# Two more tiles transposed by DMA, stores held a slot longer, and the last tile finished half by half

## The chip, the cores and the metric

The kernel runs on one core of a Trainium2 chip. The metric is the device time of one execution in microseconds (us); the time before is the median of four runs. The other times are from one execution that was taken with the hardware profiler. Engines are named as in the profile: PE is TensorE (PEld its weight loads), DVE is VectorE, ACT is ScalarE, POOL is GpSimd, SP is SyncE. SP computes nothing here: it issues nearly all the DMAs, strictly in program order, and the profile shows those issues as SPq.

## The reference, cut to what matters

Inputs are q, k and v of shape (4, 8, 768, 64): batch, heads, positions, head size. Per batch and head a decayed state is carried over the positions:

```
state = gamma[None, :, None, None] * state + np.einsum('bhd,bhe->bhde', k[:, :, t], v[:, :, t])
y[:, :, t] = scale * np.einsum('bhd,bhde->bhe', q[:, :, t], state)
```

The heads are put side by side, which gives x of shape (4, 768, 512), and x goes through a block that mixes the positions and then the channels:

```
theta = x @ w_theta
zr = x * cos(theta)
zi = x * sin(theta)
y = einsum('ts,bsd->btd', w_tok_r, zr) + einsum('ts,bsd->btd', w_tok_i, zi)
u = x + y
out = u + maximum(u @ w_ch, 0)
```

The change lies in the last two lines: `u`, its product with `w_ch`, and the store of `out`.

## The kernel before, in words

**Tiles and slots.** The first half works on pairs of 128 positions: three pairs per batch, n = 0 to 11. The second half works on tiles of 128 positions: six per batch, m = 0 to 23. The two halves are interleaved by hand in one program order: after a prologue, the loop at line 592 runs slots n = 3 to 12. Slot n computes the recurrence of pair n, finishes pair n-1, and does the position mixing (`moe_M`) of the one or two tiles in `tiles_of[n]`, called `mine`. The tiles of the slot before, `done`, get their product with `w_ch` (`moe_O`) and their output (`moe_out`). From slot 7 on there are two tiles a slot: 6 and 7 in slot 7, 8 and 9 in slot 8, 10 and 11 in slot 9, and so on to 16 and 17 in slot 12. Tiles 18 to 22 follow in the loop at line 719, and tile 23 in `moe_last` (line 407).

**The way of one tile.** `moe_M` (line 327) is 12 products of 128x512 into PSUM. `moe_u` (344) adds x on DVE and leaves `u` in bf16, with five buffers. `moe_O` (365) needs `u` transposed, as its weights, and there are two ways to get that. `moe_U` (355) transposes on PE: four 128x128 products a tile against the identity, then one ACT copy from PSUM (line 361). `moe_U_dma` (350) issues one DMA transpose from SP, with four buffers `uT`. The constant `U_DMA` (line 63) says from which slot the second way is taken: in a slot n >= `U_DMA` the second tile of `done` is sent to DMA at the head of the slot (604); in a slot n with n+1 >= `U_DMA` the first tile of `mine` is sent in the middle (666); in a slot n < `U_DMA` both tiles of `done` go through PE (676). Before, `U_DMA` is 9, so tiles 6 and 7 are the last to be transposed on PE, in slot 8. `moe_O` of the tiles of `done` stands at the end of each slot (708). `moe_out` (372) takes the maximum and the sum on DVE into `ot`, which has eight buffers.

**SP's order in a slot.** Slots 8 and 9 look like this on SP: the DMA transposes of k and q of the next pair (`flip_dma`, 598 and 600); from slot 9 on the `u` of the second tile of `done`; the transpose of x of pair n-1 (`x_dma`, 638); the loads of k, q and v of pair n+3 (640, 642 and 662; pair 11, loaded in slot 8, is the last); the stores that `stores_in(n)` names (663); the `u` of the first tile of `mine` (666). Nothing overtakes on SP.

**Stores.** `stores_in` (583) gives every slot its stores. Slots 6 to 8 store nothing; slots 9, 10 and 11 store tiles 3 to 5, 6 to 8 and 9 to 11; slot 12 stores 12 and 13. With eight buffers of `ot`, the `moe_out` of tile m waits for the store of tile m-8.

**The last tile.** `moe_last` splits tile 23. The columns 0 to 383 of `u` are transposed first and columns 384 to 511 last (`flip_u`: PE, then an ACT copy, line 430). The output is made in two halves of 256 columns, e = 0 and 1, each a sum over four products (j = 0 to 3), of which j = 3 needs the last ACT copy. Before, PE runs j = 0 to 2 of both halves and then j = 3 of both (446 to 451). DVE then finishes half 0 and half 1 (454); SP issues the store of half 0 and ACT that of half 1.

Of the kernel before, what the change touches and what calls it, by code (L numbers as in the profile page):

```python
# [32 lines left out]
def kernel(  # L33
# [17 lines left out]
    nc = tc.nc  # L51
    B, H, S, D = q.shape
# [3 lines left out]
    nT = S // P  # L56
    nD = dm // P
# [2 lines left out]
    gammas = [1.0 - 2.0 ** (-5.0 - h) for h in range(H)]  # L60
    nG = nT // 2

    K_DMA, Q_DMA, X_DMA, U_DMA = 2 * nG + 1, 3 * nG - 1, 2 * nG - 1, 3 * nG

    ctx.enter_context(tc.manual_schedule())

# [89 lines left out]
    wch = const.tile([P, nD, dm], BF)  # L156
# [193 lines left out]
    def moe_U_dma(m):  # L350
        uT = work.tile([P, nD, P], BF, name="uT", bufs=4)
        nc.sync.dma_start_transpose(out=uT, in_=mo[m]["u"])
        mo[m]["uT"] = uT
# [11 lines left out]
    def moe_O(m):  # L365
        o_ps = psum.tile([P, dm], FT, name="o_ps", tag="tr", bufs=2)
        for j in range(nD):
            nc.tensor.matmul(o_ps, mo[m]["uT"][:, j, :], wch[:, j, :], start=(j == 0),  # L368
                             stop=(j == nD - 1))
        mo[m]["o"] = o_ps  # L370

    def moe_out(m):
        b, t0 = divmod(m, nT)
        ot = work.tile([P, dm], FT, name="ot", bufs=8)
        nc.vector.scalar_tensor_tensor(ot, mo[m]["o"], 0.0, mo[m]["u"], ALU.max, ALU.add)  # L375
        mo[m]["ot"] = ot

    def store(m):
        b, t0 = divmod(m, nT)
        nc.sync.dma_start(out=out[b, t0 * P:(t0 + 1) * P, :], in_=mo[m]["ot"])  # L380
# [26 lines left out]
    def moe_last(m):  # L407

        b, t0 = divmod(m, nT)
        cut = (nD - 1) * P  # L410
        cols = (slice(0, cut), slice(cut, dm))
        y_ps = [psum.tile([P, cut], FT, name="y_ps", tag="y", bufs=1),
                psum.tile([P, P], FT, name="y_ps", tag="acc", bufs=2)]
        u = work.tile([P, dm], BF, name="u", bufs=5)
        uT = work.tile([P, nD, P], BF, name="uT", bufs=4)

        def prods(e):
            for s0 in range(nT):
                for r in range(2):
                    nc.tensor.matmul(y_ps[e], wT[r][:, s0, t0 * P:(t0 + 1) * P],  # L420
                                     zs[b][:, s0, r, cols[e]],
                                     start=(s0 == 0 and r == 0),
                                     stop=(s0 == nT - 1 and r == 1))
            nc.vector.tensor_add(u[:, cols[e]], y_ps[e], xs[b][:, t0, cols[e]])

        def flip_u(lo, hi):
            u_ps = psum.tile([P, hi - lo, P], BF, name="u_ps", tag="tr", bufs=2)
            for j in range(lo, hi):
                nc.tensor.transpose(u_ps[:, j - lo, :], u[:, j * P:(j + 1) * P], ident)  # L429
            nc.scalar.copy(uT[:, lo:hi, :], u_ps)  # L430

        moe_U_dma(m - 1)
        prods(0)
        moe_O(m - 2)
        moe_out(m - 2)
        store(m - 2)
        prods(1)
        flip_u(0, nD - 1)
        moe_O(m - 1)
        moe_out(m - 1)  # L440
        store(m - 1)
        flip_u(nD - 1, nD)
        hw = dm // 2
        o_ps = [psum.tile([P, hw], FT, name="o_ps", tag="st", bufs=1),
                psum.tile([P, hw], FT, name="o_ps", tag="acc", bufs=2)]
        for js in (range(nD - 1), (nD - 1,)):
            for e in range(2):
                for j in js:
                    nc.tensor.matmul(o_ps[e], uT[:, j, :],
                                     wch[:, j, e * hw:(e + 1) * hw], start=(j == 0),  # L450
                                     stop=(j == nD - 1))
        for e in range(2):
            ot = work.tile([P, hw], FT, name="oh", bufs=2)
            nc.vector.scalar_tensor_tensor(ot, o_ps[e], 0.0, u[:, e * hw:(e + 1) * hw],
                                           ALU.max, ALU.add)
            (nc.sync, nc.scalar)[e].dma_start(
                out=out[b, t0 * P:(t0 + 1) * P, e * hw:(e + 1) * hw], in_=ot)
# [125 lines left out]
    def stores_in(n):  # L583

        if n < 2 * nG:
            return tiles_of[n - 2]
        if n < 3 * nG:
            return []
        lo = 2 * nG - 3 + 3 * (n - 3 * nG)
        return range(lo, min(lo + 3, (B - 2) * nT + 2))  # L590

    for n in range(nG, B * nG + 1):
        mine, done = tiles_of[n], tiles_of[n - 1]
# [69 lines left out]
        for t in stores_in(n):  # L663
            store(t)
# [54 lines left out]
    for m in range(last_m - nT + 1, last_m):  # L719
# [8 lines left out]
        moe_M(m, 4, nT)  # L728
        moe_u(m)
    moe_last(last_m)  # L730
# [1 line left out]
_INS = ['q', 'k', 'v', 'moe_w_theta', 'moe_w_tok_r', 'moe_w_tok_i', 'moe_w_ch']  # L732
# [26 lines left out]
```

## Time and profile before

| what | us |
|---|---|
| median of four runs | 168.44 (167.81 to 169.4) |
| the profiled execution, its own time | 168.7 |
| its span in the trace | 167.0 |
| PE busy in the span | 156.9 (94%) |
| DVE, ACT, POOL busy | 101.8, 79.1, 64.9 |
| granted PE clock over the span | 1.0 |
| slot 8, from its first product to slot 9's | 87.37 to 98.75 |
| slot 9 | 98.75 to 109.22 |

How to read it: a time in the trace is counted from the start of the span. PE products overlap in the records, so the cost of a product in a row of products is the distance between two starts, not its own duration. The chain of waits lists what the end of the program hung on, piece by piece; there the pieces don't overlap and add up. An SPq duration is the time that SP spent on issuing that one DMA; when the data has landed is a separate figure, counted from the start of the issue.

### The profile page before, as it was taken

The page shows a single profiled execution, that of the slowest core. Times are in us where ns is not written, and L with a number is a line of the kernel's source. Part 1 is how long each engine was busy: PE and PEld are TensorE (multiplying, and loading weights), DVE is VectorE, ACT ScalarE, POOL GpSimd, SP SyncE. Part 2 cuts the span into 40 slices and gives each one's busy share as a digit, 9 for nine tenths or more (in the row PEclk, how much of TensorE's full clock was granted, in tenths as well). Part 3 has the DMA queues.
Part 4 walks back from the last instruction along what each step waited for, and adds up shares of the span by engine and source line. Part 5 has one row for each costly group of instructions (what it writes and reads, how often), then busy time and mean ns, then how long its engine had stood idle before and what let it go on. Part 6 is the DMA issues. An engine that isn't in the chain of part 4 may idle for free.

```text
span 167.0 us, 4640 instructions
## 1 busy us (share of the span) xinstructions
PE 156.9 (94%) x1959; PEld 87.5 (52%) x1959; DVE 101.8 (61%) x137; ACT 79.1 (47%) x137; POOL 64.9 (39%) x82
## 2 busy tenths in 40 slices
PE   6979897899899999999999999999999999999991
PEld 2445665664566666555555554555545444444460
DVE  2358896988686599929446464584554736334442
ACT  7216568461809557587846827447083350000010
POOL 6374859787396876681632704400000000000000
PEclk9999999999999999999999999999999999999999
DMA  4999999999999999999999999968977161743343
GB/s 129 302 345 307 326 294 363 298 331 315 310 304 304 296 294 331 307 214 278 194 225 286 162 261 205 211 181 165 271 128 195 31 188 31 227 121 96 105 139 137
DMA packets 68901, 38.45 MB, mean 230 GB/s; under 512 B 26256, under 2 KB 63376, under 8 KB 68880
## 3 DMA queue, kind: packets, MB, share of 16 engines
q1 hardware_dynamic: 68736, 38.02, 88.7%
q8 instruction: 15, 0.25, 0.7%
q10 hardware_dynamic: 144, 0.13, 0.2%
q14 instruction: 6, 0.05, 0.1%
HBM read 25.69 MB, written 6.29 MB: 192 GB/s over the span
## 4 chain that ended last, share of the span: by engine, by line
PE 66%; DMA 16%; SPq 9%; DVE 4%; issue 1%; POOL 1%; ACT 1%; DVEq 0%
PE y_ps L340 31%; PE o_ps L368 12%; DMA pair<-in_k_dram 9%; PE th_ps L312 8%; DMA pair<-in_q_dram 7%; SPq L81 5%; PE yT_ps L231 3%; PE at_ps L208 2%; PE yT_ps L245 2%; PE st_ps L262 2%; SPq L95 2%; PE y_ps L420 2%; PE kq_ps L183 1%; POOL kqb L171 1%; SPq L89 1%
## 5 line engine op out<-in xcount | busy, mean ns | idle before, releaser
L340 PE MATMUL y_ps<-z,wtr 128*128 128x512 bf16 x138 | 52.4, 380 | 0.7 <-DVE z L322 0.7
L340 PE MATMUL y_ps<-z,wti 128*128 128x512 bf16 x138 | 52.3, 379 | 0.0
L347 DVE TENSOR_TENSOR u<-y_ps,x_sb 128x512 bf16<-128x512 f32 x23 | 15.8, 689 | 26.9 <-PE y_ps L340 26.7
L215 DVE TENSOR_TENSOR at<-at_ps,maskp 128x1024 bf16<-128x1024 f32 x24 | 29.3, 1221 | 4.4 <-PE at_ps L208 4.4
L175 POOL TENSOR_TENSOR kqb<-pair,qscp 128x512 bf16<-128x512 f32 x17 | 18.4, 1098 | 30.3 <-DMA pair<-in_q_dram 30.3
L175 POOL TENSOR_TENSOR kqb<-pair,vscp 128x512 bf16<-128x512 f32 x24 | 25.8, 1097 | 5.4 <-DMA pair<-in_v_dram 4.8
L285 ACT CAST xT<-yT_ps 128x512 bf16<-128x512 f32 x20 | 13.5, 737 | 30.0 <-PE yT_ps L231 30.0
L375 DVE SCALAR_TENSOR_TENSOR ot<-o_ps,u 128x512 f32<-128x512 f32 x23 | 15.9, 691 | 13.6 <-PE o_ps L368 13.4
L312 PE MATMUL th_ps<-wth,xT 128*128 128x512 bf16 x96 | 23.3, 379 | 0.1
L368 PE MATMUL o_ps<-wch,uT 128*128 128x512 bf16 x92 | 22.8, 379 | 0.3 <-DVE ot L375 0.3
L340 PEld LDWEIGHTS <-wti 128*128 128x128 bf16 x138 | 13.5, 98 | 13.8 <-issue 0.6
L276 ACT CAST stbd<-st_ps 64x256 bf16<-64x256 f32 x40 | 14.7, 367 | 12.7 <-PE st_ps L262 12.2
L340 PEld LDWEIGHTS <-wtr 128*128 128x128 bf16 x138 | 13.5, 98 | 13.7
L315 ACT ACTIVATE cs<-th_ps,halfpi 128x512 bf16<-128x512 f32 x24 | 16.5, 688 | 7.3 <-PE th_ps L312 6.8
L322 DVE TENSOR_TENSOR z<-cs,x_sb 128x1024 bf16<-128x1024 bf16 x24 | 17.7, 760 | 0.1
L316 ACT ACTIVATE cs<-th_ps,zerob 128x512 bf16<-128x512 f32 x24 | 16.5, 687 | 0.0
L312 PEld LDWEIGHTS <-xT 128*128 128x128 bf16 x96 | 9.0, 98 | 10.6 <-ACT xT L285 0.6
L368 PEld LDWEIGHTS <-uT 128*128 128x128 bf16 x92 | 8.8, 98 | 10.4 <-issue 0.4
L430 ACT COPY uT<-u_ps 128x384 bf16<-128x384 bf16 (+1 forms) x2 | 0.7, 372 | 25.5 <-PE u_ps L429 25.5
L208 PE MATMUL at_ps<-kqT 64*64 64x128 bf16 x384 | 10.6, 221 | 2.0 <-DVE at L215 1.3
L187 DVE COPY kqT<-kq_ps 128x1024 bf16<-128x1024 bf16 x14 | 9.6, 687 | 4.6 <-PE kq_ps L183 4.4
L183 PE MATMUL kq_ps<-ident,kqb 128*128 128x128 bf16 x120 | 9.5, 222 | 1.7 <-DVE wtr L400 0.6
(61 smaller groups left out, 167.1 us busy)
## 6 DMA issues: line engine op xcount, KB each, us to landing
pair<-in_k_dram SPq DMA_DIRECT2D x12, 512.0 KB, 6.6
pair<-in_q_dram SPq DMA_DIRECT2D x12, 512.0 KB, 7.5
pair<-in_v_dram SPq DMA_DIRECT2D x12, 512.0 KB, 8.3
out_dram<-ot SPq DMA_DIRECT2D x23, 256.0 KB, 2.4
wtok<-in_moe_w_tok_r_dram SPq DMA_DIRECT2D x6, 384.0 KB, 6.3
wtok<-in_moe_w_tok_i_dram SPq DMA_DIRECT2D x6, 384.0 KB, 5.6
w<-in_moe_w_theta_dram SPq DMA_DIRECT2D x1, 1024.0 KB, 8.0
w<-in_moe_w_ch_dram SPq DMA_DIRECT2D x1, 1024.0 KB, 7.6
```

The lines of the kernel that those rows point to most:

```text
L175: engines[two].tensor_mul(dst[:, two], src[:, two], _bcast_last(sc[:, 2 * g + two], D))
L208: nc.tensor.matmul(at_ps[half, par, j, :], kT[rows, two, j, half], qT[rows, :, j, half], start=(j == 0), stop=(j == NP - 1), skip_group_ch ...
L215: nc.vector.tensor_mul(at.rearrange("p a j t -> p (a j) t"), at_ps.rearrange("p a j t -> p (a j) t"), _bcast_mid(maskp[:, two].rearrange(" ...
L276: nc.scalar.copy(stbd[(c + 1) % 2][sl, :, sl], st_ps[b][sl])
L312: nc.tensor.matmul(th_ps, st[n, "xT"][:, a, j, :], wth[:, j, :], start=(j == 0), stop=(j == NP - 1))
L315: nc.scalar.activation(cs[:, 0, :], th_ps, AF.Sin, bias=halfpi, scale=1.0)
L316: nc.scalar.activation(cs[:, 1, :], th_ps, AF.Sin, bias=zerob, scale=1.0)
L322: nc.vector.tensor_mul(zs[b][:, c], st[n, "cs", a], _bcast_mid(xs[b][:, c, :], 2))
L340: nc.tensor.matmul(y_ps, wT[r][:, s0, t0 * P:(t0 + 1) * P], zs[b][:, s0, r, :], start=(s0 == 0 and r == 0), stop=(s0 == nT - 1 and r == 1))
L347: nc.vector.tensor_add(u, mo[m]["y"], xs[b][:, t0, :])
L368: nc.tensor.matmul(o_ps, mo[m]["uT"][:, j, :], wch[:, j, :], start=(j == 0), stop=(j == nD - 1))
L375: nc.vector.scalar_tensor_tensor(ot, mo[m]["o"], 0.0, mo[m]["u"], ALU.max, ALU.add)
```

## The change

Three edits. `U_DMA` becomes 8: tile 6 is sent to DMA in the middle of slot 7, tile 7 at the head of slot 8 after the transposes of k and q, and the PE transposes with their ACT copy in slot 8 go away. Slot 9 stores nothing; slots 10 and 11 store four tiles each (3 to 6 and 7 to 10) and slot 12 three (11 to 13). In `moe_last` half 0 gets its four products first and then half 1.

```diff
-    K_DMA, Q_DMA, X_DMA, U_DMA = 2 * nG + 1, 3 * nG - 1, 2 * nG - 1, 3 * nG
+    K_DMA, Q_DMA, X_DMA, U_DMA = 2 * nG + 1, 3 * nG - 1, 2 * nG - 1, 3 * nG - 1
...
-        for js in (range(nD - 1), (nD - 1,)):
-            for e in range(2):
-                for j in js:
-                    nc.tensor.matmul(o_ps[e], uT[:, j, :],
-                                     wch[:, j, e * hw:(e + 1) * hw], start=(j == 0),
-                                     stop=(j == nD - 1))
+        for e in range(2):
+            for j in range(nD):
+                nc.tensor.matmul(o_ps[e], uT[:, j, :],
+                                 wch[:, j, e * hw:(e + 1) * hw], start=(j == 0),
+                                 stop=(j == nD - 1))
...
-        if n < 3 * nG:
+        if n <= 3 * nG:
             return []
-        lo = 2 * nG - 3 + 3 * (n - 3 * nG)
-        return range(lo, min(lo + 3, (B - 2) * nT + 2))
+        lo = 2 * nG - 3 + 4 * (n - 3 * nG - 1)
+        return range(lo, min(lo + 4, (B - 2) * nT + 2))
```

SP's order around the change, before and after (the two `u` transposes that are new are marked with a star):

```
slot 7   before  k8 q8 x6 load10(k q v)            after  k8 q8 x6 load10(k q v) u6*
slot 8   before  k9 q9 x7 load11(k q v) u8         after  k9 q9 u7* x7 load11(k q v) u8
slot 9   before  k10 q10 u9 x8 out3 out4 out5 u10  after  k10 q10 u9 x8 u10
slot 10  before  k11 q11 u11 x9 out6 out7 out8 u12 after  k11 q11 u11 x9 out3 out4 out5 out6 u12
slot 11  before  u13 x10 out9 out10 out11 u14      after  u13 x10 out7 out8 out9 out10 u14
slot 12  before  u15 x11 out12 out13 u16           after  u15 x11 out11 out12 out13 u16
```

## The prediction

> **What bounds the kernel now.** I read the page's first rows and the chain of waits, then the slots one by one, then SP's own timeline. The page says who is busy:
>
> ```profile
> PE 156.9 (94%) x1959; PEld 87.5 (52%) x1959; DVE 101.8 (61%) x137; ACT 79.1 (47%) x137; POOL 64.9 (39%) x82
> ...
> PE 66%; DMA 16%; SPq 9%; DVE 4%; issue 1%; POOL 1%; ACT 1%; DVEq 0%
> ```
>
> PE is busy 94% of the span; the DMA and SPq shares of the chain lie before 45 us. From there on PE has almost no gap, so a piece taken off PE is worth its length and a wait put on PE costs its length. Busy time of PE, PEld, DVE, ACT and POOL in slots 8 to 11 (the columns after the length):
>
> ```profile
> 87.37:98.75 11.38, 11.38 (x154) 6.24 (x153) 6.25 (x9) 7.03 (x12) 4.09 (x4) 1.00 1.16 232
> 98.75:109.22 10.47, 10.47 (x125) 5.28 (x124) 6.24 (x9) 5.53 (x9) 4.05 (x4) 1.00 1.15 230
> 109.22:120.15 10.93, 10.93 (x145) 5.79 (x144) 6.25 (x9) 5.07 (x10) 0.00 (x0) 1.00 0.81 202
> ```
>
> PE fills each of them. Slot 8 has slot 10's PE work plus the PE transposes, and is 0.45 longer. The chain inside slot 8 shows the piece that goes:
>
> ```profile
> 94.15 0.45 PE u_ps L359 x8
> 94.59 2.59 PE y_ps L340 x12
> 97.18 1.73 PE o_ps L368 x8
> ```
>
> SP's timeline from the loads of pair 10 (slot 7) to the x transpose in slot 9; start, duration of the issue:
>
> ```profile
> 83.91 0.57 SPq L81 DMA_DIRECT2D pair<-in_k_dram  x1
> ...
> 87.10 3.33 SPq L195 DMA_TRANSPOSE kqT<-kqb  x1
> 90.54 2.75 SPq L195 DMA_TRANSPOSE kqT<-kqb  x1
> 93.38 1.26 SPq L290 DMA_TRANSPOSE x_sb<-xT  x1
> 94.69 0.57 SPq L81 DMA_DIRECT2D pair<-in_k_dram  x1
> ...
> 97.41 3.77 SPq L352 DMA_TRANSPOSE uT<-u  x1
> 101.29 1.52 SPq L195 DMA_TRANSPOSE kqT<-kqb  x1
> 102.92 1.25 SPq L195 DMA_TRANSPOSE kqT<-kqb  x1
> 104.26 1.24 SPq L352 DMA_TRANSPOSE uT<-u  x1
> 105.59 1.27 SPq L290 DMA_TRANSPOSE x_sb<-xT  x1
> ```
>
> One issue follows the next within 0.1 us: SP has no slack here, and a DMA put in pushes all that stands behind it. The issue at 104.26 is u9 (tile 9's u), which slot 9's second output product needs: its weight load is the fifth of these eight.
>
> ```profile
> 107.28 1.61 PEld L368 LDWEIGHTS <-uT 128*128 128x128 bf16 x8
> ```
>
> Spacing (1.61 - 0.10)/7 = 0.216, so that load begins at 107.28 + 4 x 0.216 = 108.14. u9 lands 2.5 us after its issue began (the DMA answer), at 106.76: PE arrives 1.38 later and doesn't wait.
>
> **Part 1a, off PE.** Eight transposes in slot 8: 8 x 0.056 (start to start) = 0.45, the piece above and the difference of slots 8 and 10. Taken: -0.45. The ACT copy of 1.01 us goes too, at no gain: ACT is idle 3.15 us in the next wait. Does another wait take the place? The products of tile 9 would start at 93.98 + a little instead of 94.43, and their PSUM is free when DVE has read tile 8, at 93.04 + 0.69 = 93.73; slot 10 has the same order without transposes, and no gap. So the 0.45 reaches the end of slot 8.
>
> The Trainium skill, "TensorE: Matmul & The Clock Gate", Part 4 (PE-mode transpose), gives about 275 ns for a transpose inside a kernel; eight would be 2.2 us, an estimate that would make this part -2.2. The rows decide: one lasts 219 ns but the next starts 56 ns later.
>
> **Part 1b, onto SP.** u6 goes in at about 87.1, ahead of k9 and q9; u7 behind q9; x7, load 11, u8, k10, q10 and u9 are all behind them. How far are they pushed (call it D)? Upper bound: two issues at the unhindered 1.24 plus 0.09 between issues = 2.66. Lower bound: the first transpose after a set of loads lasts 3.3 to 3.8 us whatever it is, and ends 6.5 after the first load began (83.91 to 90.43, 94.69 to 101.18). In slot 9 that one is u8, and k10 and q10 then take 1.52 and 1.25 instead of 3.33 and 2.75: from the first load to the end of q it is 9.48 with a u in between and 9.38 without. So u6 costs 0.1; if u7 were absorbed too, D = 0.1. I take the row that is the same sequence: load, u, k, q, u, x is slot 9's now, and would be slot 8's. From first load to x it took 105.59 - 94.69 = 10.90; slot 8's without the two u took 93.38 - 83.91 = 9.47. D = 1.43.
>
> The rule of the Trainium skill, "DMA: Bandwidth & Descriptors", section "Issuing engines are not separate DMA queues", says that a sequencer's time to initiate a DMA is usually small beside the DMA itself. By it D would be near 0 and the sum -0.38. The row speaks against it: 1.24 of issue in 2.5 to landing.
>
> Who waits, then? Slot 8: u7 is issued at 83.91 + 9.57 = 93.48 and lands at 95.98; its weight load comes at 96.81 + 0.86 - 0.45 = 97.22. Covered by 1.2 (by nothing at D = 2.66). u6, at 87.1 + 6.8 (u8's landing now), lands at 93.9, wanted at 96.36. k9 and q9 are wanted at 98.6 and land by about 97. Load 11: POOL's q of pair 11 now starts at 102.32, would be 1.4 later and end by 108, wanted by SP at 111. x7 and x8 are late by D for DVE's z, which slots 10 and 11 use microseconds later.
>
> Slot 9: u9 is issued at 104.26 + D and lands at 106.76 + D. A reader starts 0.11 after a landing (q of pair 10 landed at 90.64, POOL began at 90.75): 106.87 + D. PE is there at 108.14 - 0.45 = 107.69. So PE waits D - 0.82; with D = 1.43, +0.61. This is the new wait; behind it on PE is all the rest.
>
> **Part 2, stores.** Slot 9's stores leave SP between x8 and u10: 106.91 to 110.08, 3.17 us. This more than returns D, so from u10 on SP runs about 1.7 earlier than now. In slot 10 four stores instead of three (0.4 to 0.6 more) are covered by that 1.7; in slot 11 by SP's gap before u14 (stores end at 125.35, next issue 126.54); in slot 12 by that before u16 (135.55 to 137.00). New wait: ot of tile 11 needs the store of tile 3, now in slot 10, at about 115.0, plus the slowest landing of these stores, 4.3: 119.3, against DVE's 120.35. Without that cover DVE's z and mask would wait behind it, which PE doesn't need for 3 us. Part 2: 0 (0 to +0.3).
>
> **Part 3, the end.** PE, ACT and DVE in the last tile:
>
> ```profile
> 162.34 1.04 PE L449 MATMUL o_ps<-wch,uT 128*128 128x256 bf16 x8
> 162.54 0.27 ACT L430 COPY uT<-u_ps 128x128 bf16<-128x128 bf16 x1 [0.55 <-PE u_ps L429]
> 163.30 0.76 DVE L454 SCALAR_TENSOR_TENSOR oh<-o_ps,u 128x256 f32<-128x256 f32 x2
> ```
>
> Products start 0.108 apart. Now six cover the copy, which ends at 162.81, and the seventh starts at 162.99. After, three cover it: the fourth needs the copy, a hand-over (0.06) and its weight load (0.10), so 162.97; half 0 ends as now. Half 1's four follow: the last starts at 163.40 (now 163.10) and ends at 163.71. DVE begins half 1 at 163.64 now. +0.07. Bounds: -0.02 (half 0's gain) to +0.32 (three products, nothing hidden).
>
> **Sum.** -0.45 + (D - 0.82, if positive) + 0.07. At D = 1.43: +0.23. The profiled execution took 168.7 (span 167.0, 1.7 around it) and would take 168.9; the median of the runs stands 0.26 lower, at 168.44, and becomes 168.7.
>
> **Rivals.**
> A, the transposes ride free: D below 0.82, PE never waits, the sum is -0.45 + 0.07 = -0.38 and the time 168.1. For it: u8 cost SP 0.1 net in slot 9. Against it: the DMA engines are almost idle from 92.5 to 93.5 and SP still issues, so u7's 1.3 has no transfer to hide behind.
> B, slower: both pay SP's full price. D = 2.66, PE waits 1.84 for u9, sum +1.46, time 169.9. For it: SP has no gap from 77 to 107. Against it: k10 and q10 got shorter behind u8. It crosses zero at D = 1.20, and one per cent (1.68) at D = 2.88, which needs a longer issue than the unhindered ones.
> C, the end: D as forecast, but the copy's hand-over is as slow as part 3's upper bound, 0.32 instead of 0.07; the sum is +0.48 and the time 168.9. For it: three covering products are gone. Against it: ACT and DVE start 0.04 after PE's ends (162.50 to 162.54).
>
> **How the numbers follow.** Forecast (D from 0.9 to 2.0, a small new wait in slot 9; sum -0.3 to +0.8, 168.1 to 169.2): 0.52. A: 0.20. B (D above 2.0): 0.18. C: 0.07. Other: 0.03. Range: from A less 0.2 for the medians' scatter, 167.9, to B, 169.9. One per cent, 1.7 us, is about what a measurement of this kernel tells from no change. Slower by more needs D above 2.88, a part of B: 0.06. Faster by more has no case, as the whole piece is 0.45: 0.02. Within: 0.92.
>
> **What would show it.** Slot 8 about 10.93 long with no transposes in it: part 1a. x7's issue at 94.8 and load 11 at 96.1: D. A gap on PE of about 0.6 in slot 9 in the middle of the output products, ended by the uT transpose: the new wait. No such gap: A. A gap of 1.8, or one already in slot 8 before tile 7: B. u10's issue near 108.4 instead of 110.08: part 2. DVE's second half of the last tile starting 0.07 later relative to the first: part 3. I am wrong if PE waits anywhere else, for instance at slot 10's first products for k10 or q10, which land at about 107.6 against 109.1.

## The result, and the profile after

The changed kernel takes 169.38 us (median of 44 runs, 167.76 to 171.32), the kernel before 168.45 (63 runs). The ratio is 1.0032, 95% interval [1.0017, 1.0046]: 0.54 us slower, 0.29 to 0.77, counted on 168.45. That is inside the forecast's range and inside one per cent. (The ratio compares runs on the same chip and leaves disturbed runs out, so it isn't the quotient of the two medians.)

The profiled execution took 169.96, with a span of 168.2. Part of that has nothing to do with the change. Let a slot begin where the chain of waits has the four products of line 245 at its head. Slot 8 begins at 88.41, before at 87.53: 0.88 later, although the program up to that place does the same work. So I compare from the start of slot 8 on. Busy time by slot, 8 to 11; the columns are length, PE, PEld, DVE, ACT, POOL, PE clock, DMA share, GB/s:

```profile
88.41:99.34 10.93, 10.93 (x147) 5.78 (x145) 6.25 (x8) 6.12 (x11) 4.09 (x4) 1.00 1.16 205
99.34:110.53 11.19, 10.65 (x127) 5.20 (x125) 6.25 (x8) 5.53 (x9) 4.05 (x4) 1.00 1.12 226
110.53:121.46 10.93, 10.93 (x147) 5.77 (x145) 6.34 (x8) 5.08 (x10) 0.00 (x0) 1.00 0.90 204
121.46:132.39 10.93, 10.93 (x147) 5.79 (x145) 6.25 (x8) 5.07 (x10) 0.00 (x0) 1.00 0.79 151
```

With the same boundaries slots 8 to 11 were 11.38, 10.48, 10.93 and 10.93 before. Slot 8 lost 0.45 and slot 9 gained 0.71; PE, which had no gap in slot 9 before, is now idle there (10.65 busy of 11.19). Slots 10 and 11 are untouched. The chain of waits in slot 9 now leaves PE and goes over SP and a DMA:

```profile
104.89 0.05 PE st_ps L262 x3
...
105.02 0.36 ACT stbd L276
...
105.49 1.25 SPq L195
106.73 0.05 issue
106.83 2.62 DMA uT<-u
109.44 0.05 issue
109.49 1.04 PE o_ps L368 x4
```

Line 368 at 109.49 is the output product of tile 9, and the DMA ahead of it is u9. The list of waits gives the weight load's wait and the product's:

```profile
PEld L368 <- DMA uT<-u: 1.0, 1, 1.0
...
PE o_ps L368 <- DMA uT<-u: 0.5, 1, 0.5
```

The loads themselves, to be held against the row of eight at 107.28 in the prediction:

```profile
107.71 0.74 PEld L368 LDWEIGHTS <-uT 128*128 128x128 bf16 x4
109.49 0.55 PEld L368 LDWEIGHTS <-uT 128*128 128x128 bf16 x4 [1.03 <-DMA uT<-u]
```

SP's timeline of the same stretch, start and duration of each issue:

```profile
84.87 0.58 SPq L81 DMA_DIRECT2D pair<-in_k_dram  x1
...
87.68 2.46 SPq L352 DMA_TRANSPOSE uT<-u  x1
90.25 1.66 SPq L195 DMA_TRANSPOSE kqT<-kqb  x1
92.02 2.38 SPq L195 DMA_TRANSPOSE kqT<-kqb  x1
94.48 1.22 SPq L352 DMA_TRANSPOSE uT<-u  x1
95.79 1.26 SPq L290 DMA_TRANSPOSE x_sb<-xT  x1
97.11 0.57 SPq L81 DMA_DIRECT2D pair<-in_k_dram  x1
...
99.60 4.18 SPq L352 DMA_TRANSPOSE uT<-u  x1
103.89 1.49 SPq L195 DMA_TRANSPOSE kqT<-kqb  x1
105.49 1.25 SPq L195 DMA_TRANSPOSE kqT<-kqb  x1
106.83 1.23 SPq L352 DMA_TRANSPOSE uT<-u  x1
108.15 1.26 SPq L290 DMA_TRANSPOSE x_sb<-xT  x1
109.51 1.22 SPq L352 DMA_TRANSPOSE uT<-u  x1
```

u6 (87.68) and u7 (94.48) are the two new ones. u9 is issued at 106.83, which is 18.42 after slot 8's start; before it was 104.26 - 87.53 = 16.73. So D is 1.69.

### The profile page after: what moved, and what is told of

The parts are those of the page before. It is cut to its first block, busy times and chain, and to the rows that moved or that the text cites. A ratio compares the mean times of both kernels' runs of the same rounds, so it can differ in the third digit from the quotient of the medians.

```text
span 168.2 us, 4624 instructions
## 1 busy us (share of the span) xinstructions
PE 156.4 (93%) x1951; PEld 86.3 (51%) x1951; DVE 103.6 (62%) x137; ACT 78.2 (47%) x136; POOL 65.6 (39%) x82
## 4 chain that ended last, share of the span: by engine, by line
PE 62%; DMA 18%; SPq 9%; DVE 5%; issue 1%; POOL 1%; ACT 1%; POOLq 0%; ACTq 0%
PE y_ps L340 29%; PE o_ps L368 11%; PE th_ps L312 8%; DMA pair<-in_q_dram 7%; SPq L81 5%; DMA pair<-in_k_dram 5%; DMA wtok<-in_moe_w_tok_i_dram 5%; PE yT_ps L231 2%; PE yT_ps L245 2%; PE at_ps L208 2%; PE st_ps L262 2%; PE y_ps L420 2%; SPq L95 2%; DMA uT<-u 2%; PE kq_ps L183 1%
## 5 line engine op out<-in xcount | busy, mean ns | idle before, releaser
L322 DVE TENSOR_TENSOR z<-cs,x_sb 128x1024 bf16<-128x1024 bf16 x24 | 18.4, 792 | 0.4 <-DMA x_sb<-xT 0.3
```

The source lines that it names most:

```text
L322: nc.vector.tensor_mul(zs[b][:, c], st[n, "cs", a], _bcast_mid(xs[b][:, c, :], 2))
```

## The experiments

**How they are read.** Two figures stand for each kernel: the timed ratio to the kernel before, and four readings of its one profile. These are u9's issue counted from slot 8's start; PE's wait for it (the weight load's, from the list of waits, which counts from the end of the load before); the length of slot 9; and the time from slot 8's start to the end of DVE's last instruction, against the 76.53 of before. The last one leaves out the scatter of the beginning: slot 8 began between 86.30 and 88.63 in the profiles, which alone is 1.4%.

| kernel | u9 issued | PE waits | slot 9 | from slot 8 to the end | timed ratio, interval |
|---|---|---|---|---|---|
| before | 16.73 | none | 10.48 | 76.53 | 1 |
| changed | 18.42 | 1.0 | 11.19 | +0.24 | 1.0032 [1.0017, 1.0046] |
| e12, changed again | 18.51 | 1.0 | 11.18 | +0.23 | 1.0012 [0.9982, 1.0042] |
| e1, DMA alone | 17.69 | 0.2 | 10.47 | -0.45 | 1.0055 [1.0028, 1.0081] |
| e2, stores alone | 16.10 | none | 10.48 | 0.00 | 0.9994 [0.9969, 1.0019] |
| e3, last tile alone | 16.81 | none | 10.47 | -0.02 | 1.0008 [0.9979, 1.0037] |
| e4, tile 6 alone by DMA | 18.89 | 1.2 | 11.31 | +0.61 | 1.0002 [0.9969, 1.0035] |
| e11, tile 6 alone again | 17.07 | none | 10.47 | -0.22 | 0.9999 [0.9968, 1.0030] |
| e5, v behind u9 | 17.63 | none (0.5 for u7) | see below | +0.91 | 1.0032 [1.0000, 1.0063] |
| e6, one transpose more | 19.08 | 1.5 | 11.70 | +0.75 | 1.0093 [1.0055, 1.0131] |
| e7, old last tile | 18.55 | 1.2 | 11.33 | +0.41 | 1.0048 [1.0011, 1.0086] |
| e8, before, v behind u9 | 16.30 | none | 10.48 | 0.00 | 0.9991 [0.9962, 1.0020] |
| e9, v behind x8 | 17.21 | none | 10.47 | -0.48 | 0.9999 [0.9968, 1.0029] |
| e10, u9 on PE | no DMA | none (0.2 for u7) | 10.68 | -0.25 | 1.0008 [0.9978, 1.0038] |

The theory under test (queue theory): two more issues on SP push u9 back, and PE waits for it. Its rivals: the four stores in a row cost the time, or the order of the last tile does.

### One part of the change at a time: e1, e2, e3

e1 is the first line of the diff on the kernel before, e2 the change of `stores_in`, e3 the change of the last tile's loops; each diff is a hunk of the one shown above.

> Tiles 6 and 7 by DMA alone; stores and last tile as before. Queue theory (u9 is pushed back on SP by 1.5 to 1.7 us and PE waits for it): slot 8 shorter by 0.45, PE waits 0.7 to 1.0 for u9 in slot 9, time +0.3 to +0.5 against before, as the whole change. Store theory (the four stores in a row are what costs): no loss here, -0.4. Tail theory (the last tile's order is what costs): -0.4 too.

> The stores held and issued four a slot, alone. Queue theory: 0 within 0.2, no new wait on PE. Store theory: +0.5 or more, with a wait of DVE for an ot buffer or of PE for a late u.

> The last tile's halves one after the other, alone. Queue theory: +0.05 to +0.1, PE waits about 0.2 to 0.3 for the last ACT copy and DVE's second half starts that little later. Tail theory: +0.3 or more.

Stores alone and last tile alone do nothing that can be measured, and nothing that the profiles show. The DMA part alone is slower by at least 0.28% in the timed runs. So the two rivals fall: what costs is in the first hunk. (e3's timed interval, up to 1.0037, would not exclude the tail theory by itself; its profile does, and so does e7 below.) But e1 is also a miss. Its timed loss, 0.93 us (0.47 to 1.36), is larger than the +0.3 to +0.5 expected, and its single profile doesn't show a loss at all. There u9 came with a D of only 0.96, PE's load waited 0.2, slot 9 was no longer than before, and the stretch from slot 8 on was 0.45 shorter, as was expected for the two other theories:

```profile
PEld L368 <- DMA uT<-u: 0.2, 1, 0.2
```

That execution was late at slot 8 already (88.63), so its total of 169.44 still fits its median of 169.31. u9 was 0.73 earlier than in the changed kernel's profile, although SP's order up to u9 is the same: 0.43 of it because SP was further ahead of PE. Its lead (the first load of pair 10 ahead of slot 8) was 3.97 there and 3.54 in the changed kernel's profile; over all the profiles it lies between 2.00 and 3.97. How large the wait is in e1's other executions isn't known; this disagreement stays open.

### The dose: e6 and e7, and the changed kernel again

e6 puts one more DMA transpose on SP, behind u7. Its result is used by nobody.

```diff
         if n >= U_DMA:
             moe_U_dma(done[1])
+            if n == U_DMA:
+                spare = work.tile([P, nD, P], BF, name="spare", bufs=1)
+                nc.sync.dma_start_transpose(out=spare, in_=mo[done[1]]["u"])
```

> The changed kernel with one useless DMA transpose more behind u7 (u of tile 7 once more, into a buffer that nobody reads). Queue theory: D grows by the issue's 1.3, PE's wait in slot 9 from 1.0 to 2.3, time +1.3 over the changed kernel, +1.7 against before. If the wait doesn't hang on the place in SP's queue: under +0.5 over the changed kernel.

```profile
PEld L368 <- DMA uT<-u: 1.5, 1, 1.5
```

In this profile the direction is right and the size too large. From the load of k of pair 10 to x7, SP needed 12.21 instead of 10.92, 1.29 more as expected; but from the load of pair 11 to u9 it needed 9.32 instead of 9.72, and it had started 0.22 earlier against PE. So u9 was 0.66 later than in the changed kernel and the wait 0.5 longer. (The 9.32 isn't shown to come from the extra transpose: without it, e7 has 9.38 and e12 9.46.) The timed runs agree with the forecast better than the profile does: against before they are 1.57 us slower (0.93 to 2.21), where +1.7 was expected, and about 1.0 slower than the changed kernel, with wide intervals. The profiled execution, at 169.63, was a quick one for a median of 170.8.

e7 is the changed kernel with the old loops of the last tile, e12 the changed kernel itself.

> The changed kernel with the last tile in the old order. Queue theory: +0.2 to +0.5 against before, 0 to 0.1 less than the changed kernel. Tail theory: the loss goes, -0.4 to 0 against before.

> The changed kernel itself in another execution, to see how much the wait for u9 moves between executions of one program. Queue theory: u9 is issued 17.7 to 19.1 after slot 8's start and PE waits that figure less about 17.5, so 0.2 to 1.5; slot 8 again 10.93. If the wait were fixed by the program alone: 1.0 again, to 0.1.

e7 keeps the wait and the loss, so the last tile isn't the cause. e12 repeats the wait of 1.0 to the tenth; e7, the same program up to the last tile, has 1.2, and e1, with the same order of issues up to u9, had 0.2, so the program alone doesn't fix it. Over all kernels with both u on SP and the loads in their place, the wait follows u9's issue: 17.69, 18.42, 18.51, 18.55 and 19.08 after slot 8's start give 0.2, 1.0, 1.0, 1.2 and 1.5, each within 0.2 of the issue less 17.55. That is the prediction's formula, D - 0.82 with 16.73 added to D. Slot 9 grew by about 0.3 less than the load's wait each time: by nothing in e1, 0.70 and 0.71 in e12 and the changed kernel, 0.85 in e7 and 1.22 in e6.

### Half the dose: tile 6 alone by DMA (e4, e11)

```diff
-        if n + 1 >= U_DMA:
+        if n + 2 >= U_DMA:
             moe_U_dma(first)
...
         if n < U_DMA:
-            moe_U(done)
+            moe_U(done[1:] if n + 1 == U_DMA else done)
```

> Only tile 6 goes by DMA, tile 7 stays on PE; stores and last tile as before. Queue theory with a u hidden behind the loads (it costs SP 0.1 net): no wait for u9, slot 8 shorter by 0.22, time -0.2. If u6 costs SP its whole 1.3 instead: u9 lands at 108.2 for a weight load at 107.9, a wait of 0.3, time +0.1.

> Tile 6 alone by DMA once more, since its first profile caught an execution in which SP was already 1.6 late against PE before the edit. Queue theory: with SP's usual lead (first load of pair 10 about 3.6 ahead of slot 8) u9 comes in time, no wait, -0.2. If a wait shows again with that lead, u6 costs SP more than the 0.16 that its first profile shows from the load of k of pair 10 to x7.

e4 timed 1.0002 [0.9969, 1.0035]. Its profile missed what was expected: SP issued the first load of pair 10 only 2.00 ahead of slot 8 (before 3.62), which the edit can't have caused, and PE waited 1.2. That execution took 170.31, for a median of 168.83. In e11, the same kernel, the lead was 3.71, and no wait showed. What u6 costs SP is read from e11, from the load of k of pair 10 to x7:

```profile
83.69 0.58 SPq L81 DMA_DIRECT2D pair<-in_k_dram  x1
...
86.44 2.43 SPq L352 DMA_TRANSPOSE uT<-u  x1
88.97 1.70 SPq L195 DMA_TRANSPOSE kqT<-kqb  x1
90.78 2.53 SPq L195 DMA_TRANSPOSE kqT<-kqb  x1
93.40 1.27 SPq L290 DMA_TRANSPOSE x_sb<-xT  x1
```

From first to last start that is 9.71 against 9.47 before: u6 costs SP 0.24, although its issue lasts 2.43, because k9 and q9 take 4.23 instead of 6.08. But 9.47 is a long one. e2, e3 and e8, whose order up to x7 is that of before, took 9.01, 9.07 and 8.95; against them u6 costs 0.64 to 0.76. No wait, slot 8 shorter by 0.22 (11.16). u7, in the changed kernel, brings the same distance to 10.92: 1.21 more, the length of its issue. So the first u hides in good part behind the loads and the second doesn't. The gain of 0.2 is seen in the profile and not resolved in the timed runs.

### Taking the cause away: e5, e8, e9, e10

e5 moves one load out of u9's way: v of pair 11 is issued in slot 9 behind u9, ahead of x8. e8 does the same to the kernel before.

```diff
         if n >= U_DMA:
             moe_U_dma(done[1])
+        if n + 2 == B * nG - 1:
+            load(n + 2, "v")
...
-        if n + 3 in pairs:
+        if n + 4 in pairs:
             load(n + 3, "v")
```

> The changed kernel, with the load of v of pair 11 issued behind u9 instead of ahead of u8. Queue theory: u9 is issued at least 1.1 earlier, and up to 3 with the load's share of the queue gone; PE's wait in slot 9 goes, and the full piece shows: -0.4 against before, -0.7 to -0.9 against the changed kernel. If u9 is late for another reason than its place behind the loads: PE's wait stays and the time is as the changed kernel's, +0.3 to +0.5.

> The kernel before with the same load of v moved behind u9; control of the late load. Queue theory: PE doesn't wait for u9 before, so an earlier u9 is worth nothing, 0 within 0.2. If the late load by itself frees something else, -0.2 or more; if v comes too late for slot 11, a new wait there and a loss.

e5 missed. u9 came 0.8 earlier and PE's wait for it is gone, but two others took its place. The small one is in slot 8 (11.06 instead of 10.93), for u7, whose order on SP is that of the changed kernel; SP's lead was only 2.55 in this execution:

```profile
95.54 1.24 SPq L352 DMA_TRANSPOSE uT<-u  x1
...
98.08 0.55 PEld L368 LDWEIGHTS <-uT 128*128 128x128 bf16 x4 [0.45 <-DMA uT<-u]
```

The large one is in slot 10. The chain from x8's issue on:

```profile
107.64 6.28 DMA x_sb<-xT
...
114.62 0.68 DVE z L322
115.30 1.15 DVE at L215
116.45 0.04 issue
116.49 0.42 PE at_ps L208 x16
```

x8 now stands behind 512 KB and lands after 6.28 us instead of the changed kernel's 3.3. DVE's z waits 3.7 for it. PE waits for that z (0.6 in the list of waits); behind z in DVE's queue is the mask of line 215, and PE needs the one PSUM buffer that the mask frees (0.2 more). PE stands in slot 10 instead of slot 9, and the stretch is 0.91 longer. In e8 x8 takes 6.3 too, but lands 1.3 earlier against slot 8, and PE loses nothing.

e9 puts the load behind x8 too, where slot 9's load of v has its place in the loop.

```diff
-        if n + 3 in pairs:
+        if n + 4 in pairs:
             load(n + 3, "v")
+        elif n + 2 == B * nG - 1:
+            load(n + 2, "v")
```

> The changed kernel with the load of v of pair 11 behind u9 and behind x8, in front of u10. Queue theory: u9 issued some 2 us earlier relative to PE than in the changed kernel, no wait for it; x8 no longer stands behind the load, so DVE's z comes in time and no wait takes its place. Slot 9 back to 10.5, time -0.4 against before. If the load merely moves the wait again: PE waits in slot 10 for u11 or in slot 11 for v, and the time stays at +0.3 or more.

```profile
86.60 0.22 PE yT_ps L245 x4
...
97.53 0.22 PE yT_ps L245 x4
106.28 1.73 PE o_ps L368 x8
108.00 0.22 PE yT_ps L245 x4
114.29 0.33 PE yT_ps L245 x4
117.21 1.73 PE o_ps L368 x8
118.94 0.22 PE yT_ps L245 x4
```

Now the chain stays on PE: slot 8 is 10.93, slot 9 10.47, slot 10 10.94. The piece taken off PE arrives at the end: -0.48 from slot 8 on. (u9 came 1.2 earlier than in the changed kernel, not 2.) The timed ratio, 0.9999 with an interval of 0.3% to either side, can't tell -0.28% from nothing.

e10 keeps everything and takes tile 9 off SP instead:

```diff
-        if n >= U_DMA:
+        if n >= U_DMA and n != U_DMA + 1:
             moe_U_dma(done[1])
...
+        if n == U_DMA + 1:
+            moe_U(done[1:])
```

> The changed kernel with tile 9 transposed on PE in slot 9, so that nothing on PE waits for u9 by DMA. Queue theory: slot 8 shorter by 0.45, slot 9 longer by 0.22 for its four transposes and free of the wait, time -0.1 to -0.2 against before. If another late transfer (x8, k10 or q10) is the real limit of slot 9: a wait of 0.5 or more stays there and the time is +0.2 or more.

```profile
103.26 0.33 PE u_ps L359 x4
106.18 1.73 PE o_ps L368 x8
107.91 0.22 PE yT_ps L245 x4
```

No wait for a DMA remains in slot 9 (in slot 8 the load for u7 waited 0.2, with SP's lead at 2.52, but slot 8 still took 10.93); slot 9 is longer by its four transposes, as expected, and the stretch is 0.25 shorter. So no other late transfer limited slot 9. Neither e9 nor e10 is shown to be faster than the kernel before. In their profiles both take away the wait; the timed runs alone don't prove it, as e9's interval reaches 1.0029 and e10's 1.0038, and the changed kernel's begins at 1.0017.

## Why the prediction was right, point by point

- **Part 1a, -0.45: as forecast.** Slot 8 went from 11.38 to 10.93 in every profile without the eight transposes (only e5 has 11.06), and nothing took their place there. "TensorE: Matmul & The Clock Gate" (the Trainium skill, Part 4, PE-mode transpose), with its 275 ns, would by the prediction's estimate have made this 2.2; the runs agree with the distance of 56 ns.
- **Part 1b, D: mechanism right, size 0.26 short.** Forecast 1.43, measured 1.69. From the first load to x7 it was 10.92 for 10.90 forecast. The rest, which the prediction set to nothing, came behind that: 9.72 instead of 9.57 from load 11 to u9, and SP's lead over PE was 0.08 smaller. That it came so close is in part luck: the 9.47 taken for the old order was a long one, and with the 8.95 to 9.07 of e2, e3 and e8 the same working would have given 0.4 to 0.5 more. Nor did u6 cost only 0.1; it was 0.24 to 0.76.
- **u7's cover of 1.2: less than it looked.** It held in the changed kernel's profiles. In e5 and e10, with the same order up to u7 but a lead of 2.5 instead of 3.62, PE's load waited for u7 in slot 8. The prediction took SP's lead from one profile.
- **The new wait: place and form right, 0.71 on slot 9 for 0.61.** At D = 1.69 the formula says 0.87. The fifth load was due at 107.71 + 4 x 0.216 = 108.57 and began at 109.49, 0.92 late (the list's 1.0 has the usual 0.12 between two loads in it). Of these 0.92 only 0.71 reached the length of slot 9. Before, a load began 0.21 ahead of its product (107.28 and 107.50); the late load and its product began together, at 109.49, so that 0.21 was cover too. The prediction took the load's delay for PE's, and left this term out.
- **The Trainium skill's rule** in "DMA: Bandwidth & Descriptors" (Issuing engines are not separate DMA queues), that the time to initiate a DMA is usually small beside the DMA, doesn't hold here: u9's issue took 1.23 of the 2.62 to its landing, and u7's, of 1.22, moved x7 by 1.21. u6's issue, of 2.46, wasn't small either; it moved what stood behind it by less (0.24 to 0.76) because k9 and q9 then took less, as the row had shown for slot 9.
- **Part 2, 0: right.** u10 was issued at 109.51, which is 108.63 on the clock of before, for 108.4 forecast; e2 shows 0.00 and 0.9994.
- **Part 3, +0.07: mis-sized by 0.09, and of the wrong sign.** The end of the changed kernel:

```profile
163.48 1.24 PE L448 MATMUL o_ps<-wch,uT 128*128 128x256 bf16 x8
163.68 0.27 ACT L430 COPY uT<-u_ps 128x128 bf16<-128x128 bf16 x1 [0.55 <-PE u_ps L429]
164.32 0.86 DVE L453 SCALAR_TENSOR_TENSOR oh<-o_ps,u 128x256 f32<-128x256 f32 x2
```

  Eight products take 1.24 instead of 1.04, so PE does wait 0.2 for the copy. But half 0's fourth product comes about 0.1 earlier against the first than its seventh slot did (hand-over and weight load together cost about 0.1, where I had 0.16), and DVE starts half 0 0.84 after PE's first product instead of 0.96. The two halves then take 0.86 for 0.76. From the twelve products of line 420 to DVE's end it is 3.40, before 3.42: -0.02. Rival C is out.
- **Rivals A and B.** A needed D below 0.82; the lowest in a kernel with both u on SP and the loads in place was 0.96, in e1. With the 0.21 of cover that was enough for slot 9 to lose nothing, so that one execution went as A says. B needed D above 2.0; it took e6's extra transpose to get to 2.35.
- **The sum.** +0.23 forecast; +0.24 and +0.23 in two profiles from slot 8 on. That this fits to 0.01 is luck. The wait was too small by 0.1 (D 0.26 short, against 0.21 of cover left out) and the end too dear by 0.09, and these cancel. The timed +0.54 (0.29 to 0.77) lies above what these two profiles show, and the forecast's +0.23 is just below that interval. Nor do the timed e9 and e10 (-0.02 and +0.13 us) show the gains of their profiles, though their intervals allow them. These differences, and e1's, I can't account for from single profiles; their cause stays open. The wait varies by execution, and so does the beginning.

## What to carry to other kernels

Where the issuing queue has no gap, a DMA put in costs its issue time to every later DMA up to the next gap; look for the first reader behind it whose cover is smaller than that, and not only at the reader of the DMA itself. The same issue can cost a good deal less than its length behind big loads, where issues are slow in any case, and its full length behind another transpose. Look at more than one profile for the cover: the issuing queue's lead over the engine it feeds changed by 2 us between executions. When a wait is taken away by moving a load, follow what now stands behind the load: e5 moved the wait from PE's weights to DVE's z, e9 one place further on removed it.

## What the runs showed of the hardware that I had not expected

- A DMA transpose of 128x1024 bf16 right behind one 512 KB load landed after 6.28 us (e5; 6.3 in e8). Behind a transpose the same one took 3.1 to 3.4 in most profiles, and 4.9 to 5.2 in e6, e7 and e12.
- An issue behind three loads lasted between 2.4 and 4.2 us, whichever transpose it was: u6 2.4 to 2.7, k9 3.3, u8 2.4 to 4.2.
- The start of slot 8 spread over 2.3 us between executions (86.30 to 88.63) with the same work ahead of it, more than four times the change's effect.
